# Splitting the expert weight loads into halves of 64 partitions, and taking out 54 products of the unit matrix

## The chip, the cores and the metric

The kernel runs on one core of a Trainium2 chip. Everything is float32. The metric is the device time of one execution in microseconds; the median of three executions before the change is 313.94 us (313.89 to 318.01).

## What is computed

Two blocks follow each other. The first is a DeltaNet recurrence over 768 steps for 4 batches and 8 heads of dimension 48; the second takes its output as 3072 rows of 384 numbers and runs a soft mixture of 8 experts with 4 slots each.

```python
# q, k, v: (4, 8, 768, 48), beta: (4, 8, 768)
for t in range(S):
    y[:, :, t] = einsum('bhd,bhde->bhe', q[:, :, t], state)
    v_old = einsum('bhde,bhd->bhe', state, kt)            # kt: k normalised
    state = state + bt * einsum('bhd,bhe->bhde', kt, vt - v_old)
# x: (3072, 384) from y; phi: (384, 32); w1: (8, 384, 1024); w2: (8, 1024, 384)
logits = x @ phi
d = softmax of logits over the rows;  slot_input = d.T @ x     # 8 experts x 4 slots
slot_out[e] = relu(slot_input[e] @ w1[e]) @ w2[e]
out = (softmax of logits over the slots) @ slot_out
```

## The kernel before

The recurrence is cut into 24 chunks of 32 steps. Six groups of four chunks each are inverted together: `prep` transposes k and q on TensorE (line 533) and forms the Gram products (line 490), `invert` runs an elimination on VectorE (lines 773 and 786), and for the first group a two-halves form with small products (lines 665 and 678). `chunk` then runs the scan: the reads of the state R and Q (line 857), the solve W (line 888), the state update KU (line 903) and the outputs AU (line 934), with copies out of PSUM on ScalarE or VectorE (the helper at lines 326 and 328). Four small DMAs for each chunk (line 945) move the copied outputs Y into X, the tile with one row for each step; there are three Y buffers. After each fourth chunk `route` transposes X (line 961), forms the logits and accumulates the slot inputs (line 1029).

`experts` comes last: the first products with w1 (line 1177), relu, transposes (line 1196), the second products with w2 (line 1208), one product that sums over the parts (line 1225), and 24 output products (line 1237), each scaled on ScalarE or VectorE and stored (line 1250). The second products run over eight parts t of the hidden dimension, four experts beside each other.

The weights are 25 MB. `weights(e)` loads w1 of one expert in three DMAs, each of 128 partitions with 4 KB for each partition (line 1084); `weights2(e)` loads w2 of one expert in four DMAs of 128 partitions with 3 KB each (line 1092). That makes 24 + 32 loads, 29 issued by POOL and 27 by SP. Their buffers ("wt") lie in one large SBUF tile, the arena, in places where the scan's buffers lie earlier: a load can only start when the last user of every buffer under it is done.

The order of all work is written out by hand: every call of `op` gets a number, and `ORDER` lists these numbers, with a letter where the second of an operation's possible engines is meant. `Plan.place` walks through this list once, gives each value its buffer or its PSUM bank, and the program is emitted in that order. So each engine, and each engine's DMA queue, runs its instructions in the order of this list; nothing is reordered later except for what semaphores delay.

At the end of the list of operations stand 54 products of the unit matrix with itself (`warm`, line 1274), numbers 1642 to 1695. Their result is read by nobody. `ORDER` puts 44 of them among the first 533 of its 1696 numbers and the other ten into the routing and expert stage. Each is written as one product and becomes two weight loads and two passes on TensorE.

Of the kernel before, what the change touches and what calls it, by code (L numbers as in the profile page):

```python
# [159 lines left out]
42b 73 8b 9b 31 6b 74 40b 7b 29b 19 1 5b 28 75 368 84 54b 66 10b 72 52b 20 67 1642 1643 1644  # L160
1645 1646 1647 64b 369 377 65b 55b 15b 378 370 87 379 371 86 386 85 372 32b 395 380 381 387 388
396 397 382 1648 1649 1650 1651 1652 76b 1653 1654 78b 77 389 398 373 383 89 390 399 374 404 79b
21 98 409 91 110 88b 99 90 47b 405 406 97 375 22 384 391 392 407 376 385 400 410 411 412 413 414
415 416 417 401 481 393 101b 12b 483 489 482 102b 418 113 96 419 420 1655 1656 421 484 402 485
403 490 422 115b 394 423 109 491 486 487 424 425 426 488 427 492 493 1657 100 494 495 428 103b
429 497 496 499 498 430 431 432 433 434 114b 108 111 112b 500 1658 1659 1660 124b 507 122 120
135 126b 505 501 127b 123 125 508 137b 442 506 509 34b 121 594 502 503 510 435 58b 14 133 44 132
511 150b 161b 436 513 595 437 514 592 438 439 408 440 441 35b 443 444 593 148b 46b 151 144 596
597 1661 1662 1663 1664 1665 1666 1667 1668 1669 445 598 512 139 599 448 446 504 515 136 518 516
520 174 519 463 472 521 522 466 523 464 475 56 524 525 526 527 528 529 530 45 33b 57b 531 1670  # L170
1671 1672 1673 1674 1675 454 532 517 533 467 68 449 145 534 535 457 447 450 451 473 160b 536 537
465 538 468 469 539 476 474 540 541 542 543 455 544 477 478 545 546 458 547 134 548 549 459 550
149 146 175b 456 83 138 602 1048 1036 600 1676 1677 1678 1679 452 453 603 1037 17 71 601 1038
629 460 604 605 551 1039 606 162 552 147 1040 607 610 1041 1042 462 1049 59b 553 554 555 80 1680
1681 1682 1050 163b 556 557 558 559 560 461 561 562 563 564 565 566 16 156 158 567 187b 157 608
186b 568 569 570 1051 159 470 197 1043 69b 609 480 70 1056 618 571 611 81b 616 92 1052 479 104b
94 619 1045 1057 617 173 1532 1058 471 612 620 1060 613 621 614 572 82 622 209b 573 199 1053
210b 624 574 625 168 575 1063 623 170 626 1047 576 615 1683 1055 1054 1116 184 106 577 1059 196
1064 1065 171 578 1078b 169 1066 579 580 581 1684 582 1067 1068 583 1069 627 631 1070 630 632
633 634 635 1071 95b 1072 105 585 636 1044 1079 1080 208b 637 638 116 1062 639 587 1081 640 641  # L180
642 643 584 93b 644 645 646 647 589 211 182 648 181 1082 649 650 651 652 185b 1685 131 1061 1073
703 1083 586 107b 128 1086 183 1087 653 119b 1085 1084 1117 1118 654 655 656 192 117b 657 1076
658 659 660 661 662 663 1131 713 664 665 666 172b 1046 1077 193 1088 1119 740 704 180 130b 705
1120 706 1121 194 714 1123 1122 707 1124 708 709 1132 198 1133 667 129 710 668 195 142 669 670
671 672 673 674 675 1146 628 590 1125 118 222b 207 140 143b 206 1134 155b 721 719 676 205 1135
233 711 23 204 221 1126 677 678 722 1136 712 246b 1074 588 1137 715 247 716 717 679 718 1075
1089 1139 220b 680 720 219 1140 727 729 681 1138 141 1141 728 1147 723 730 682 683 684 1091 1090
591 1092 685 1148 686 1200b 217 1128 724 687 731 732 165 725 726 1161 223 1149 1097 1150 152b
153b 1144 733 1129 1098 688 735 736 167b 689 690 1151 1152 1093 734 1095 154 1153 1094 1096 166b
691 692 693 232 229 1533 231 1154 1127 234b 1162 1099 737 694 1163 1215b 696 698 695 1100b 1101  # L190
738 741 742 164 1102 743 230 744 745 746 747 748 749 750 751 1164 176 1130 739 752 816 1109 753
1110 216 1165 700 1166 697 228 218 817 1168 256b 241 754 1111 235b 1169 1155 177b 1170 178 1167
755 756 240 1143 1201 1156 1202 243 242 814 189b 1158 757 758 759 760 761 1142 762 763 764 765
766 1230 822 1203 767 768 1171 188b 815 270b 1204 1174 818 823 819 245b 701 824 1172 1205 1208
820 769 825 257 1175 283b 821 1209 1207 770 1145 1206 1216 1173 1245 771 1217 252 259b 826 244b
254 772 773 774 775 255 1159 776 1218 777 778 1210 830 827 779 828 1219 780 829 1157 258b 201b
1220 781 1223 1103 699 782 1160 783 784 785 786 787 788 831 1224 1180 1105 1178 1222 1221 1225
832 1181 1231 1112 179b 1106 253 1176 1212 1179 190b 266 840 833 265 838 1232 789 1113 790 791
214b 702 792 294b 1177 841 839 292b 282 1233 293 793 1234 271b 794 268 795 834 835 836 842 843
1235 796 851 1228 844 797 846 191 1236 1237 279 202 1284 847 845 1229 798 837 799 800 1246 1107  # L200
269b 1182 1247 801 295 1211 281b 802 1248 848 803 1108 804 805 267 1299 1183 1184 849 852 853
1185 1249 854 855 856 857 203 858 850 859 860 861 862 1238 1250 927 1253 807 1254 1252 1251 806
1285 1226 278 1286 863 864 865 866 867 1186 868 869 870 871 872 873 1214 874 875 876 877 1239
307 305 277 200 928 808 264 276 809 225b 811 1227 1287 925 1288 926 1289 1240 288 289 280 290
1255 1292 929 1291 304b 933 1293 1290 930 1213 291 878 931 301 879 934 1300 932 880 1301 881 882
215b 883 884 885 303 886 887 888 1314 889 306b 890 1242 891 237 1294 941 935 1189 942 1241 302
1302 936 1243 300 937 1303 1304 1190 1244 250b 226 938 939 1114 892 940 943 1115 212b 1306 1307
1305 1308 962 893 239b 894 895 1315 896 1316 897 249b 898 899 900 213 901 227 238 1296 944 810
813 949 1257 248 951 1317 1309 950 952 902 945 1318 236b 251b 812 903 904 946 1258 947 905 953
954 955 1398 906 224 957 1319 262 907 313 1320 958 908 956 909 1321 1256 1329b 1193 1368 910 948  # L210
911 1194 912 1195 1383 1259 913 959 1330 1331 914 915 916 960 963 964 965 966 967 968 969 970
971 972 1322 1332 1260 1333 917 1297 1261 1334 1336 1335 275 1264 1262 973 1323 1369 974 1324
1370 975 976 977 978 979 980 981 316b 918 1337 1371 272b 982 317 1312 983 984 985 986 987 988
274 961 1263 1265 1372 1373 1298 989 990 1375 261 312b 1313 1295 1266 1374 1376 1384 1385 1311
991 992 1267 1268 993 994 995 996 315b 997 998 999 1000 1001 1187 1310 1377 1002 1269 1003 1196
1004 920 919 314b 1328 922 1386 1338 1387 1327 1326 921 1388 287b 1339 1005 286 1389 319b 1390
1270 1325 1391 263 1191 1399 260b 320b 1006 285b 1342 1400 1378 1392 1007 1008 1341 1340 1009
1010 1011 1192 1012 1013 1014 296b 1413 1401 1402 1403 1343 1404b 1393 299 1273 924 1015 1346
1016 1406 1017 1018 273b 1405 923 1414 1415 1019 298b 1020 1021 1022 1023 1024 1025 297b 1380
1407 1381 1416 1452 1026 1274 309b 1408 1348 1417 1027 1347 1418 1382 308 1419 1275 1420b 1379  # L220
310 1421 318 1349b 1029b 1453 1454 1031 1422 1028 1032 1394 1396 284 1271 1035 1455 1030b 321
1423b 1034b 1344 1456 1457 324 1467b 1395 1412 328 1411 1460 330b 1345b 1350 323 1458b 1397 1459
1033 329b 311b 1468 1351 325b 1104 1461 1352 1409 1469 1470 1475 1462 1410 1353 1471 1427 1482b
1354 1472 1476 1473 1357 1424 1358 1474b 327b 331b 1425 332b 1426 326b 1463 1466 1483 1359 1484
322 1477 1497b 1485 1490 1355 1486b 1276 1487 1488b 1478 1491 1489 1428 1492b 1498 1432 1430
1431 1499 1197 1500 1502 1481 1479 335 1501b 1433b 1503 1429b 1464 1361 1465 1504 1480 1434 1495
1505 1435b 1506 1507 334 333 338 1496 1445 1494 1436 1493 339b 336 1437 1438 1686 1277 1512 1439
1508 1510 337 1441 1360 1513b 1509b 1687 1688 1511 1278 1514 1515 1516 1517 1525 1442 1443 1518
1521 343b 1519 1534 342 1444 1535 341b 1536 1522 1537 1538 1689 1690 1691 1692 340b 345b 1523
1524 1541 1198 1693 1694 346b 344 1695 350 353b 1542b 349 351 354 347 1545 355 352 348 1543 357b  # L230
363b 359b 367b 358 1546 1544 1547 356 1188 360 1279 365 364b 361b 1549 1553 1272 1526 1280 1548
1282 1551 1550b 1559 1356 1560 1440 362 1199b 366b 1446 1281 1552 1362 1554 1555 1557 1556b 1561
# [10 lines left out]
def kernel(  # L243
# [12 lines left out]
    P = 128  # L256
# [4 lines left out]
    NWARM = 54  # L261
# [1078 lines left out]
```

## Time and profile before

| | value |
|---|---|
| median of three executions | 313.94 us |
| profiled execution | 322.0 us, of which 320.2 us from its first to its last instruction |
| mean granted TensorE clock in it | 0.894 of full speed |
| TensorE matmul / weight loads busy | 268.8 us (84%) / 216.4 us (68%), 6080 each |
| VectorE, ScalarE, POOL busy | 221.2 us (69%), 191.0 us (60%), 119.3 us (37%) |
| line 1084 (w1) loads, issue on POOL / on SP | 11 of 531 ns / 13 of 445 ns (medians) |
| line 1092 (w2) loads, issue on POOL / on SP | 18 of 537 ns / 14 of 428 ns (medians) |
| line 1084 / 1092, issue to landing | median 6.8 us (3.9 to 10.3) / 8.5 us (4.6 to 14.8) |
| line 1274, unit-matrix products | 108 passes, 19.5 us busy |

In the profile PE is TensorE's matmul side and PEld its weight loads; DVE is VectorE, ACT ScalarE, POOL GpSimd and SP SyncE. A "q" behind an engine's name means its sequencer, which issues DMAs. A matmul's end is modelled, so the busy time of PE overstates its work. The clock is given as a share of full speed, and the DMA share is the mean busy share of the core's 16 DMA engines[...]. The chain of waits follows the work that ended last back to what released it, step by step; "issue" in it is time in which the engine waited for nothing that the profile shows.

### The profile page before, as it was taken

To read this page: it belongs to the slowest core of one execution; us is meant where nothing else is said; L and a number is where in the kernel's file an instruction comes from. 1 tells how busy PE (TensorE), PEld (TensorE's weight loads), DVE (VectorE), ACT (ScalarE), POOL (GpSimd) and SP (SyncE) were. 2 spreads that over 40 slices of the span, in tenths; PEclk is the share of its full clock that TensorE was granted. 3 is DMA by queue.
4 is the path that set the end of the run, shared out by engine and by line. 5 is a ranking of instruction groups with operands and counts; after the bars stand their busy time and mean duration, and the time that the engine had idled before them with its cause. 6 is when DMAs were issued, how large, how long until landed. Compare 5 with 4: busy or idle time off the path is not lost.

```text
span 320.2 us, 14453 instructions
## 1 busy us (share of the span) xinstructions
PE 268.8 (84%) x6080; PEld 216.4 (68%) x6080; DVE 221.2 (69%) x609; ACT 191.0 (60%) x473; POOL 119.3 (37%) x252
## 2 busy tenths in 40 slices
PE   4998689959899899995999597698798988899890
PEld 4887578857778778884878586576686875333460
DVE  5489996797689999999799999847532544012530
ACT  2545565883799898987798887386442132211362
POOL 8659492126614274445405162222000234300032
PEclk9999956995999999996999989789986999999955
DMA  8968511343555546644528249959992699993195
GB/s 129 154 120 165 90 42 35 58 76 58 96 88 100 99 69 118 114 81 76 102 42 162 49 107 265 217 104 323 316 279 49 198 354 398 377 356 147 68 326 198
DMA packets 87472, 49.66 MB, mean 155 GB/s; under 512 B 77280, under 2 KB 79200, under 8 KB 87408
## 3 DMA queue, kind: packets, MB, share of 16 engines
q1 hardware_dynamic: 78176, 28.41, 40.0%
q0 software_dynamic: 7056, 19.93, 21.8%
q8 instruction: 48, 0.79, 1.1%
q10 hardware_dynamic: 2176, 0.39, 0.9%
q14 instruction: 16, 0.13, 0.1%
HBM read 39.47 MB, written 4.72 MB: 138 GB/s over the span
## 4 chain that ended last, share of the span: by engine, by line
PE 57%; DVE 18%; ACT 8%; issue 7%; DMA 6%; POOL 2%; SPq 0%; POOLq 0%; ACTq 0%; DVEq 0%
PE banks L857 9%; PE banks L888 6%; PE banks L903 6%; PE banks L934 5%; PE banks L490 5%; ACT arena L326 5%; DMA arena<-in_moe_w_dram 4%; PE banks L533 4%; PE banks L1274 4%; PE banks L1237 4%; DVE arena L696 3%; PE banks L961 2%; DVE arena L773 2%; DVE arena L786 2%; PE banks L1177 2%
## 5 line engine op out<-in xcount | busy, mean ns | idle before, releaser
L326 ACT ACTIVATE arena<-banks 64x384 f32<-64x384 f32 (+4 forms) x205 | 98.8, 505 | 71.8 <-PE banks L903 22.1
L786 DVE TENSOR_TENSOR arena<-arena 128x31 f32<-128x31 f32 (+15 forms) x155 | 53.1, 343 | 4.2
L773 DVE TENSOR_TENSOR arena<-arena 128x60 f32<-128x60 f32 (+9 forms) x150 | 52.0, 347 | 3.9
L452 POOL DMA_DIRECT2D arena<-in_v_dram x49 | 28.7, 589 | 59.3 <-DVE arena L773 23.0
L857 PE MATMUL banks<-arena 128*32 128x96 f32 x1440 | 44.6, 271 | 6.2 <-DVE arena L509 3.6
L857 PEld LDWEIGHTS banks<-arena 128*32 128x32 f32 x1440 | 35.1, 121 | 12.7 <-issue 7.9
L452 POOL DMA_DIRECT2D arena<-in_q_dram x58 | 33.8, 588 | 14.7 <-PE banks L533 14.1
L328 DVE COPY arena<-banks 64x384 f32<-64x384 f32 (+3 forms) x24 | 13.6, 577 | 31.8 <-PE banks L1196 13.9
L888 PE MATMUL banks<-arena 64*64 64x48 f32 x768 | 29.7, 230 | 5.6 <-issue 2.3
L888 PEld LDWEIGHTS banks<-arena 64*64 64x64 f32 x768 | 27.1, 146 | 10.5 <-issue 3.5
L903 PE MATMUL banks<-arena 32*128 32x96 f32 x736 | 29.4, 296 | 5.0 <-issue 3.0
L533 PE MATMUL banks<-ident,arena 128*128 128x128 f32 x192 | 29.4, 292 | 4.6 <-DVE par L392 4.6
L846 ACT ACTIVATE arena<-arena,nTall 128x48 f32<-128x48 f32 x136 | 32.1, 322 | 0.1
L903 PEld LDWEIGHTS banks<-arena 32*128 32x128 f32 x736 | 25.0, 199 | 9.5 <-issue 4.5
L934 PE MATMUL banks<-arena 64*64 64x48 f32 x736 | 27.8, 227 | 3.1 <-issue 3.1
L562 ACT ACTIVATE arena<-arena,par 128x256 f32<-128x256 f32 x45 | 29.8, 698 | 0.3 <-DVE arena L790 0.2
L934 PEld LDWEIGHTS banks<-arena 64*64 64x64 f32 x736 | 25.0, 142 | 6.4 <-issue 4.1
L490 PE MATMUL banks<-arena 64*64 64x128 f32 (+1 forms) x896 | 26.2, 261 | 2.5 <-DVE arena L509 1.5
L533 PEld LDWEIGHTS banks<-ident,arena 128*128 128x128 f32 x192 | 22.2, 148 | 7.1 <-issue 5.3
L490 PEld LDWEIGHTS banks<-arena 64*64 64x64 f32 x896 | 22.1, 136 | 4.8 <-ACT arena L326 3.3
L878 DVE TENSOR_TENSOR arena<-arena,banks 128x384 f32<-128x384 f32 x23 | 12.6, 549 | 16.0 <-PE banks L857 10.2
L1274 PE MATMUL banks<-ident 128*128 128x128 f32 x108 | 19.5, 332 | 4.3 <-DVE arena L509 3.5
(141 smaller groups left out, 349.9 us busy)
## 6 DMA issues: line engine op xcount, KB each, us to landing
arena<-in_moe_w_dram POOLq DMA_DIRECT2D x18, 384.0 KB, 8.2
arena<-in_moe_w_dram SPq DMA_DIRECT2D x13, 512.0 KB, 7.4
arena<-in_moe_w_dram POOLq DMA_DIRECT2D x11, 512.0 KB, 5.8
arena<-in_moe_w_dram SPq DMA_DIRECT2D x14, 384.0 KB, 9.3
arena<-arena SPq DMA_DIRECT2D x92, 48.0 KB, 3.2
arena<-in_k_dram SPq DMA_DIRECT2D x88, 48.0 KB, 3.0
out_dram<-arena SPq DMA_DIRECT2D x15, 192.0 KB, 2.1
arena<-in_q_dram POOLq DMA_DIRECT2D x58, 48.0 KB, 3.1
```

The lines of the kernel that those rows point to most:

```text
L326: AC.activation(dst, src, ACT.Copy)
L452: dge[e].dma_start(out=sb(x, U, pad)[hs[h], :, 0:D], in_=src.rearrange("b (g h) s d -> h s (b g) d", h=4)[h, cc * C:(cc + 1) * C])
L490: PE.matmul(t[hp_[hp], g, b * P:b * P + m], lhsT=kt[rs_[g], b, 0, h2].rearrange("p h t -> p (h t)"), rhs=rhs, start=True, stop=True, skip_ ...
L533: PE.transpose(t[:, b, :], m[:, b, :], ident)
L773: nc.vector.tensor_tensor(o.rearrange("p (i k) -> p i k", k=m), t[:, j, 0:m].unsqueeze(1).broadcast_to([P, a1 - a0, m]), s[:, i, j].unsque ...
L786: nc.vector.tensor_tensor(d, d, o, op=ALU.subtract)
L846: AC.activation(t[:, b, g], t[:, b, g], ACT.Copy, scale=f[:, b, g:g + 1])
L857: PE.matmul(t[hs[h], b], lhsT=m[:, b, a, hs[h]], rhs=s[:, h, b], start=(a == 0 or b == 0), stop=False, skip_group_check=True)
L888: PE.matmul(t[hp_[i], b, g], lhsT=m[hp_[i], g, b], rhs=r[hp_[i], b, g], start=True, stop=True, skip_group_check=True)
L903: PE.matmul(banks[:, h, b * G * D:(b + 1) * G * D], lhsT=m[hs[h], b], rhs=r[hs[h], b], start=(cc == 0 and b == 0), stop=True, skip_group_c ...
L934: PE.matmul(t[hp_[i], b, g], lhsT=m[hp_[i], g, b], rhs=r[hp_[i], b, g], start=(cc == 0 and b == 0 and g == 0), stop=True, skip_group_check ...
L1274: PE.matmul(ps(wm, P), lhsT=ident, rhs=ident, start=True, stop=True)
```

## The change

Each weight load is issued as two DMAs, one for partitions 0 to 63 and one for 64 to 127, one after the other on the same queue. The number of unit-matrix products is set to zero, and their numbers are taken out of `ORDER`; the order of the other numbers is the same.

```diff
-1645 1646 1647 64b 369 377 65b 55b 15b 378 370 87 379 371 86 386 85 372 32b 395 380 381 387 388
-396 397 382 1648 1649 1650 1651 1652 76b 1653 1654 78b 77 389 398 373 383 89 390 399 374 404 79b
...
+42b 73 8b 9b 31 6b 74 40b 7b 29b 19 1 5b 28 75 368 84 54b 66 10b 72 52b 20 67 64b 369 377 65b
+55b 15b 378 370 87 379 371 86 386 85 372 32b 395 380 381 387 388 396 397 382 76b 78b 77 389 398
...
-    NWARM = 54
+    NWARM = 0
...
         for i in range(NKT):
             def ld(eng, i=i, x=x):
-                dge[eng].dma_start(out=sb(x, NKT, F)[:, i],
-                                   in_=moe_w1[e].rearrange("(p k) f -> p k f", k=NKT)[:, i])
+                for h in (slice(0, 64), slice(64, P)):
+                    dge[eng].dma_start(out=sb(x, NKT, F)[h, i],
+                                       in_=moe_w1[e].rearrange("(p k) f -> p k f", k=NKT)[h, i])
...
         for i in range(4):
             def ld(eng, i=i, x=x):
-                dge[eng].dma_start(out=sb(x, NFC, Dm)[:, 2 * i:2 * i + 2],
-                                   in_=moe_w2[e].rearrange("(p t) d -> p t d", t=NFC)[
-                                       :, 2 * i:2 * i + 2])
+                for h in (slice(0, 64), slice(64, P)):
+                    dge[eng].dma_start(out=sb(x, NFC, Dm)[h, 2 * i:2 * i + 2],
+                                       in_=moe_w2[e].rearrange("(p t) d -> p t d", t=NFC)[
+                                           h, 2 * i:2 * i + 2])
```

Lines after the list move up by three in the new file, and those below the first load by one or two.

More of the change, by code (lines that the diff above doesn't have):

```diff
@@ L159 @@
 24b 4b 13b 25 27b 26 2b 3b 18b 37b 38 39b 11b 36 50b 63 60 51b 0 48b 49b 61 62 30b 43b 41b 53b
-42b 73 8b 9b 31 6b 74 40b 7b 29b 19 1 5b 28 75 368 84 54b 66 10b 72 52b 20 67 1642 1643 1644
-1645 1646 1647 64b 369 377 65b 55b 15b 378 370 87 379 371 86 386 85 372 32b 395 380 381 387 388
-396 397 382 1648 1649 1650 1651 1652 76b 1653 1654 78b 77 389 398 373 383 89 390 399 374 404 79b
-21 98 409 91 110 88b 99 90 47b 405 406 97 375 22 384 391 392 407 376 385 400 410 411 412 413 414
-415 416 417 401 481 393 101b 12b 483 489 482 102b 418 113 96 419 420 1655 1656 421 484 402 485
@@ L165 @@
[L165 to L230, printed above, removed]
@@ L231 @@
-363b 359b 367b 358 1546 1544 1547 356 1188 360 1279 365 364b 361b 1549 1553 1272 1526 1280 1548
-1282 1551 1550b 1559 1356 1560 1440 362 1199b 366b 1446 1281 1552 1362 1554 1555 1557 1556b 1561
-1558 1562 1563 1564 1565 1566 1363 1520 1364 1539 1567 1366 1365 1540 1283 1568 1569 1570 1573
-1576 1582 1447 1367b 1448 1450 1579 1571 1574b 1451b 1577 1580 1572 1588 1597 1585 1578 1575b
-1600 1591 1583 1594 1581 1449 1586 1603 1615 1589b 1590 1592 1595 1606 1609 1612 1598b 1601 1527
-1599 1621 1587b 1584 1528 1624 1618 1604b 1607 1530 1627 1610 1529 1613 1602 1531 1593 1616b
@@ L237 @@
-1619 1608 1605b 1636 1630 1622b 1639 1596b 1623 1625b 1628 1631 1633 1614b 1611b 1634 1620 1637
-1640 1635b 1632b 1641 1638 1629 1626 1617b
+42b 73 8b 9b 31 6b 74 40b 7b 29b 19 1 5b 28 75 368 84 54b 66 10b 72 52b 20 67 64b 369 377 65b
+55b 15b 378 370 87 379 371 86 386 85 372 32b 395 380 381 387 388 396 397 382 76b 78b 77 389 398
+373 383 89 390 399 374 404 79b 21 98 409 91 110 88b 99 90 47b 405 406 97 375 22 384 391 392 407
+376 385 400 410 411 412 413 414 415 416 417 401 481 393 101b 12b 483 489 482 102b 418 113 96 419
@@ new lines @@
+420 421 484 402 485 403 490 422 115b 394 423 109 491 486 487 424 425 426 488 427 492 493 100 494
+495 428 103b 429 497 496 499 498 430 431 432 433 434 114b 108 111 112b 500 124b 507 122 120 135
+126b 505 501 127b 123 125 508 137b 442 506 509 34b 121 594 502 503 510 435 58b 14 133 44 132 511
+150b 161b 436 513 595 437 514 592 438 439 408 440 441 35b 443 444 593 148b 46b 151 144 596 597
+445 598 512 139 599 448 446 504 515 136 518 516 520 174 519 463 472 521 522 466 523 464 475 56
+524 525 526 527 528 529 530 45 33b 57b 531 454 532 517 533 467 68 449 145 534 535 457 447 450
@@ new lines @@
+451 473 160b 536 537 465 538 468 469 539 476 474 540 541 542 543 455 544 477 478 545 546 458 547
+134 548 549 459 550 149 146 175b 456 83 138 602 1048 1036 600 452 453 603 1037 17 71 601 1038
+629 460 604 605 551 1039 606 162 552 147 1040 607 610 1041 1042 462 1049 59b 553 554 555 80 1050
+163b 556 557 558 559 560 461 561 562 563 564 565 566 16 156 158 567 187b 157 608 186b 568 569
+570 1051 159 470 197 1043 69b 609 480 70 1056 618 571 611 81b 616 92 1052 479 104b 94 619 1045
+1057 617 173 1532 1058 471 612 620 1060 613 621 614 572 82 622 209b 573 199 1053 210b 624 574
@@ new lines @@
+625 168 575 1063 623 170 626 1047 576 615 1055 1054 1116 184 106 577 1059 196 1064 1065 171 578
+1078b 169 1066 579 580 581 582 1067 1068 583 1069 627 631 1070 630 632 633 634 635 1071 95b 1072
+105 585 636 1044 1079 1080 208b 637 638 116 1062 639 587 1081 640 641 642 643 584 93b 644 645
+646 647 589 211 182 648 181 1082 649 650 651 652 185b 131 1061 1073 703 1083 586 107b 128 1086
+183 1087 653 119b 1085 1084 1117 1118 654 655 656 192 117b 657 1076 658 659 660 661 662 663 1131
+713 664 665 666 172b 1046 1077 193 1088 1119 740 704 180 130b 705 1120 706 1121 194 714 1123
@@ new lines @@
+1122 707 1124 708 709 1132 198 1133 667 129 710 668 195 142 669 670 671 672 673 674 675 1146 628
+590 1125 118 222b 207 140 143b 206 1134 155b 721 719 676 205 1135 233 711 23 204 221 1126 677
+678 722 1136 712 246b 1074 588 1137 715 247 716 717 679 718 1075 1089 1139 220b 680 720 219 1140
+727 729 681 1138 141 1141 728 1147 723 730 682 683 684 1091 1090 591 1092 685 1148 686 1200b 217
+1128 724 687 731 732 165 725 726 1161 223 1149 1097 1150 152b 153b 1144 733 1129 1098 688 735
+736 167b 689 690 1151 1152 1093 734 1095 154 1153 1094 1096 166b 691 692 693 232 229 1533 231
@@ new lines @@
+1154 1127 234b 1162 1099 737 694 1163 1215b 696 698 695 1100b 1101 738 741 742 164 1102 743 230
+744 745 746 747 748 749 750 751 1164 176 1130 739 752 816 1109 753 1110 216 1165 700 1166 697
+228 218 817 1168 256b 241 754 1111 235b 1169 1155 177b 1170 178 1167 755 756 240 1143 1201 1156
+1202 243 242 814 189b 1158 757 758 759 760 761 1142 762 763 764 765 766 1230 822 1203 767 768
+1171 188b 815 270b 1204 1174 818 823 819 245b 701 824 1172 1205 1208 820 769 825 257 1175 283b
+821 1209 1207 770 1145 1206 1216 1173 1245 771 1217 252 259b 826 244b 254 772 773 774 775 255
@@ new lines @@
+1159 776 1218 777 778 1210 830 827 779 828 1219 780 829 1157 258b 201b 1220 781 1223 1103 699
+782 1160 783 784 785 786 787 788 831 1224 1180 1105 1178 1222 1221 1225 832 1181 1231 1112 179b
+1106 253 1176 1212 1179 190b 266 840 833 265 838 1232 789 1113 790 791 214b 702 792 294b 1177
+841 839 292b 282 1233 293 793 1234 271b 794 268 795 834 835 836 842 843 1235 796 851 1228 844
+797 846 191 1236 1237 279 202 1284 847 845 1229 798 837 799 800 1246 1107 269b 1182 1247 801 295
+1211 281b 802 1248 848 803 1108 804 805 267 1299 1183 1184 849 852 853 1185 1249 854 855 856 857
@@ new lines @@
+203 858 850 859 860 861 862 1238 1250 927 1253 807 1254 1252 1251 806 1285 1226 278 1286 863 864
+865 866 867 1186 868 869 870 871 872 873 1214 874 875 876 877 1239 307 305 277 200 928 808 264
+276 809 225b 811 1227 1287 925 1288 926 1289 1240 288 289 280 290 1255 1292 929 1291 304b 933
+1293 1290 930 1213 291 878 931 301 879 934 1300 932 880 1301 881 882 215b 883 884 885 303 886
+887 888 1314 889 306b 890 1242 891 237 1294 941 935 1189 942 1241 302 1302 936 1243 300 937 1303
+1304 1190 1244 250b 226 938 939 1114 892 940 943 1115 212b 1306 1307 1305 1308 962 893 239b 894
@@ new lines @@
+895 1315 896 1316 897 249b 898 899 900 213 901 227 238 1296 944 810 813 949 1257 248 951 1317
+1309 950 952 902 945 1318 236b 251b 812 903 904 946 1258 947 905 953 954 955 1398 906 224 957
+1319 262 907 313 1320 958 908 956 909 1321 1256 1329b 1193 1368 910 948 911 1194 912 1195 1383
+1259 913 959 1330 1331 914 915 916 960 963 964 965 966 967 968 969 970 971 972 1322 1332 1260
+1333 917 1297 1261 1334 1336 1335 275 1264 1262 973 1323 1369 974 1324 1370 975 976 977 978 979
+980 981 316b 918 1337 1371 272b 982 317 1312 983 984 985 986 987 988 274 961 1263 1265 1372 1373
@@ new lines @@
+1298 989 990 1375 261 312b 1313 1295 1266 1374 1376 1384 1385 1311 991 992 1267 1268 993 994 995
+996 315b 997 998 999 1000 1001 1187 1310 1377 1002 1269 1003 1196 1004 920 919 314b 1328 922
+1386 1338 1387 1327 1326 921 1388 287b 1339 1005 286 1389 319b 1390 1270 1325 1391 263 1191 1399
+260b 320b 1006 285b 1342 1400 1378 1392 1007 1008 1341 1340 1009 1010 1011 1192 1012 1013 1014
+296b 1413 1401 1402 1403 1343 1404b 1393 299 1273 924 1015 1346 1016 1406 1017 1018 273b 1405
+923 1414 1415 1019 298b 1020 1021 1022 1023 1024 1025 297b 1380 1407 1381 1416 1452 1026 1274
@@ new lines @@
+309b 1408 1348 1417 1027 1347 1418 1382 308 1419 1275 1420b 1379 310 1421 318 1349b 1029b 1453
+1454 1031 1422 1028 1032 1394 1396 284 1271 1035 1455 1030b 321 1423b 1034b 1344 1456 1457 324
+1467b 1395 1412 328 1411 1460 330b 1345b 1350 323 1458b 1397 1459 1033 329b 311b 1468 1351 325b
+1104 1461 1352 1409 1469 1470 1475 1462 1410 1353 1471 1427 1482b 1354 1472 1476 1473 1357 1424
+1358 1474b 327b 331b 1425 332b 1426 326b 1463 1466 1483 1359 1484 322 1477 1497b 1485 1490 1355
+1486b 1276 1487 1488b 1478 1491 1489 1428 1492b 1498 1432 1430 1431 1499 1197 1500 1502 1481
@@ new lines @@
+1479 335 1501b 1433b 1503 1429b 1464 1361 1465 1504 1480 1434 1495 1505 1435b 1506 1507 334 333
+338 1496 1445 1494 1436 1493 339b 336 1437 1438 1277 1512 1439 1508 1510 337 1441 1360 1513b
+1509b 1511 1278 1514 1515 1516 1517 1525 1442 1443 1518 1521 343b 1519 1534 342 1444 1535 341b
+1536 1522 1537 1538 340b 345b 1523 1524 1541 1198 346b 344 350 353b 1542b 349 351 354 347 1545
+355 352 348 1543 357b 363b 359b 367b 358 1546 1544 1547 356 1188 360 1279 365 364b 361b 1549
+1553 1272 1526 1280 1548 1282 1551 1550b 1559 1356 1560 1440 362 1199b 366b 1446 1281 1552 1362
@@ new lines @@
+1554 1555 1557 1556b 1561 1558 1562 1563 1564 1565 1566 1363 1520 1364 1539 1567 1366 1365 1540
+1283 1568 1569 1570 1573 1576 1582 1447 1367b 1448 1450 1579 1571 1574b 1451b 1577 1580 1572
+1588 1597 1585 1578 1575b 1600 1591 1583 1594 1581 1449 1586 1603 1615 1589b 1590 1592 1595 1606
+1609 1612 1598b 1601 1527 1599 1621 1587b 1584 1528 1624 1618 1604b 1607 1530 1627 1610 1529
+1613 1602 1531 1593 1616b 1619 1608 1605b 1636 1630 1622b 1639 1596b 1623 1625b 1628 1631 1633
+1614b 1611b 1634 1620 1637 1640 1635b 1632b 1641 1638 1629 1626 1617b
```

## Prediction

> **What bounds the kernel now.** I read the page's clock and DMA rows first, then the busy times in stretches of 4 us, then the chain of waits, and last the DMA issues of the tail. The profiled execution took 322.0 us (span 320.2), 2.6% above the median of 313.94; I work out differences in it and add them to the median.
>
> From the page: the granted clock and the DMA share in 40 slices of 8 us, the unit-matrix products, and the queue that brings instructions.
>
> ```profile
> PEclk9999956995999999996999989789986999999955
> DMA  8968511343555546644528249959992699993195
> ...
> L1274 PE MATMUL banks<-ident 128*128 128x128 f32 x108 | 19.5, 332 | 4.3 <-DVE arena L509 3.5
> ...
> q8 instruction: 48, 0.79, 1.1%
> ```
>
> The products (54, each recorded as two passes) are 19.5 us of TensorE time. The clock halves in slices 6, 10 and the last two. Memory is loaded in slices 22 to 36, where the weights arrive. Stretches of 4 us (PE, weight loads, DVE, ACT, POOL busy; clock; DMA share; GB/s):
>
> ```profile
> 40.00:44.00 4.00, 3.25 (x41) 3.14 (x41) 3.52 (x11) 2.30 (x7) 3.94 (x6) 0.56 0.21 43
> 52.00:56.00 4.00, 4.00 (x77) 3.60 (x78) 1.74 (x5) 1.09 (x2) 1.90 (x4) 0.73 0.25 53
> ...
> 72.00:76.00 4.00, 3.27 (x60) 2.70 (x61) 2.38 (x8) 1.34 (x6) 3.18 (x11) 0.50 0.38 62
> ...
> 204.00:208.00 4.00, 2.68 (x47) 2.58 (x46) 3.43 (x10) 0.49 (x1) 0.00 (x0) 0.54 1.10 216
> ...
> 268.00:272.00 4.00, 3.26 (x30) 2.33 (x29) 2.02 (x8) 0.17 (x1) 2.46 (x5) 1.00 1.04 408
> ```
>
> VectorE is at least 85% busy in most stretches from 16 to 52 us and from 92 to 208: it bounds the scan. TensorE decides where VectorE has holes (52 to 92) and from 208 on. From 255 the loads of w2 run beside TensorE's last stage at about 400 GB/s. The chain (start, length):
>
> ```profile
> 41.37 2.86 PE banks L1274 x12
> ...
> 52.16 1.71 PE banks L1274 x8
> ...
> 202.24 3.08 issue
> ...
> 227.13 2.33 issue
> ...
> 239.55 2.06 issue
> ...
> 278.76 13.78 DMA arena<-in_moe_w_dram
> 292.58 4.71 PE banks L1208 x55
> ```
>
> The last load of w2 ends at 292.5, and the second products, the fold and 24 stores hang on it. It is a near tie: TensorE itself stood only 0.5 us before 292.58. The three "issue" pieces lie about 127 passes, or a multiple of that, apart; 127 passes are 254 instructions. The DMA view of 252 to 292.6 us:
>
> ```profile
> DMA packets 4969, 14.40 MB, mean 355 GB/s; under 512 B 1646, under 2 KB 1646, under 8 KB 4963
> ...
> arena<-in_moe_w_dram POOLq DMA_DIRECT2D x18, 384.0 KB, 8.2
> arena<-in_moe_w_dram SPq DMA_DIRECT2D x14, 384.0 KB, 9.3
> ```
>
> [...] after TensorE's idle at 68 to 72 us the next stretches are at 0.50. [...]
>
> **The split.** 29 POOL loads and 27 SP loads become 58 and 54 of half the size. Bytes and order stay.
>
> *Issue.* POOL: 29 x 0.54 us = 15.6 us more, SP: 27 x 0.43 = 11.6. POOL has nothing behind its last loads before the store at 302 us, but its last five (277.6 to 280.2) become ten and end near 283. Both queues then issue 384 KB in 1.07 us (POOL) and 0.86 us (SP), together 800 GB/s, twice what lands: hidden by the transfers themselves; without that cover it costs 2.7 us. On SP the moves L945 and v loads queue behind the w1 parts, each 0.43 us later per part; the waits for them are ACT's output copies (three Y buffers) and L961. In the compiled instruction list a queue's DMA waits for the one eight before it, so half as many bytes are in flight per queue; 8 x 192 KB on two queues is 3 MB, 7.9 us at 400 GB/s, as much as a load takes now: nothing.
>
> *Rate.* Unknown[...]. The two queues are at different places, so an even half on one may run beside an odd half on the other. [...]
> - Tail: 14.40 MB take 51.4 us instead of 40.6: +10.8 (0 to +26). Of it about 3.3 return: the last load, of two of the eight parts t of one expert, is needed by 16 of the 55 passes that now follow it (2 parts x 4 experts x 2 passes), and the others can go ahead (4.71 x 39/55). TensorE then waits in pieces, with a halved clock now and then: +1. Net +8.5 (0 to +24).
> - w1 stage, 186 to 252 us: 23 parts (12.06 MB) and 57 transfers of 48 KB. At 166 GB/s (the stretch 8 to 12 us, small transfers only, engines full) the small ones need 17 us; the weights 30 us at 400, 43 at 280[...]. Sum 47, 60 or 73 of 66 us. At 280 the slack is nearly gone, so moves, v loads and instruction blocks come later here and there: I take +3 (-5 to +10; the gain is below).
>
> **The removal.** 216 instructions and 108 passes go from TensorE; the PSUM bank of every other product stays as it was. *Gain:* on the chain lie 12.8 us of them (4.0%), but what follows decides. The 12 at 5.7 us free transposes whose copy waits for ACT until 7.5: under 1 us. Those of 12 to 40 us lie beside VectorE's unbroken work: 0; next late is VectorE. Those at 41.4, 52.2 and 60.1 (2.86 + 1.71 + 0.86) are before the first chunks, where VectorE stands idle 4.0 us in 52 to 62: at most 4 us. Those of 261 to 272 lie beside the w2 transfers: 0. *Cost:* [...] At 5.7 us a pass took 213 ns (2.56/12) and at 27.9 us 112 ns (0.67/6), though the clock row shows 1.00 at both: I read the start as half rate, too. The rate doubled while they ran, so without them TensorE may stay at half rate for a stretch longer at the start and around 52. A chunk at half clock is 4 us dearer (L888 1.95 for 0.93, L903 1.97 for 1.07, L857 twice 1.44 for 0.80, L934 1.88 for 1.06). The trace also shows recovery by chunk work alone in about 5 us (147 to 152, 206 to 210). Range -4 to +5; I take -1.
>
> **Sum:** 8.5 + 3 - 1 = +10.5 us, 322.0 to 332.5 in the profiled terms, and 313.9 to **325 us** for the median.
>
> **Rivals.**
> - [...] +24 in the tail, +7 in the w1 stage (73 - 66), -1: +30, **344 us**. [...]
> - *No limit:* 400 GB/s stay, issue is hidden, clock cost and gain cancel: **314 us**. [...]
> - *Faster, by shorter blocking.* The stalls of 0.97, 3.08, 0.97, 2.33 and 2.06 us from 197 to 242 (9.4 us) are instruction blocks behind weights. If an engine finishes one load's share before it turns to the block, halves cut this wait to half: -4.7, and the halved clock after each stall (0.54 at 204 to 208) goes too, -1; with the products' 3 us: **305 us**. It decides only if the rate stays above about 350 GB/s; below it the queue is longer and eats the gain.
> - *The change acts on the clock alone*, more than I take: +5, 319 us.
>
> **How the numbers follow.** Middle rate 0.43 (316 to 334), [...] no limit with the clock case 0.18 (309 to 321), shorter blocking 0.12 (301 to 308). A measurement of this kernel tells about 2% from no change: 307.7 and 320.2. Slower: 0.27 + 0.33 of the middle case + 0.02 = 0.62. Same: 0.10 + 0.11 + 0.02 = 0.23. Faster: 0.05 + 0.10 = 0.15. The range is 307 to 346, leaving out about 0.12 below and 0.08 above.
>
> **What would show it.** Right: w2's transfers at 220 to 320 GB/s with a DMA share near 1, the last load landing 8 us or more after the end of the first products' first half than now, and PE waits for weights before L1207 (L1208 now). Wrong: 400 GB/s in the tail (then the rivals with the rate kept); "issue" pieces under 1 us between 190 and 250 (shorter blocking); clock stretches of 0.50 before 60 us longer than now with VectorE waiting for TensorE there (the clock cost is larger than I took).

## Result and the profile after

The changed kernel took **345.23 us** (median of 4 executions, 343.29 to 346.32) beside 315.98 us for the kernel before (median of 4): 29 us more, a ratio of 1.096 (95% interval 1.090 to 1.101). The forecast was 325 us; the time lies at the upper end of its range, where the rival at 344 us put it.

The profiled execution took 343.29 us (span 341.4). Executions of one kernel differ by some per cent, the ratio compares the quicker ones of both kernels, and the profiled one of before, 322.0 us, was a long one: the two profiles differ by 21.3 us and the medians by 29.2. The page of the changed kernel: clock, DMA share and GB/s in 40 slices (8.5 us each), then the second products of the experts and the w2 loads (busy us, mean ns of one, then idle time before them and what ended most of it), last the two queues' w2 issues (count, KB each, median us to landing).

```profile
PEclk9998656967999999999996976969899989678995
DMA  8978511444555455345571999999999999998087
GB/s 134 140 127 139 84 39 27 78 74 75 101 96 107 74 108 107 72 78 98 92 136 19 217 194 173 194 217 221 208 209 216 226 242 250 241 239 206 2 298 256
...
L1091 POOL DMA_DIRECT2D arena<-in_moe_w_dram x36 | 18.8, 525 | 29.2 <-DMA arena<-in_moe_w_dram 21.9
...
L1207 PE MATMUL banks<-arena 128*32 128x384 f32 x128 | 16.1, 613 | 16.0 <-DMA arena<-in_moe_w_dram 16.0
...
arena<-in_moe_w_dram POOLq DMA_DIRECT2D x36, 192.0 KB, 10.1
...
arena<-in_moe_w_dram SPq DMA_DIRECT2D x28, 192.0 KB, 16.4
```

The DMA share stands at 0.9 or more in 14 slices in a row, and in all of them less than 255 GB/s are moved; before, the page has 354 to 398 in four slices of the tail. Half the bytes of a load now take longer to land than the whole took (10.1 and 16.4 us against 8.2 and 9.3). TensorE waits 16.0 us for weights ahead of its second products, where it waited 0.5 us:

```profile
L1208 PE MATMUL banks<-arena 128*32 128x384 f32 x128 | 11.5, 488 | 0.5 <-DMA arena<-in_moe_w_dram 0.5
```

Stretches of 4 us of the changed kernel (PE, weight loads, DVE, ACT, POOL; clock; DMA share; GB/s):

```profile
252.00:256.00 4.00, 2.99 (x62) 2.33 (x59) 2.04 (x6) 0.40 (x2) 2.55 (x5) 1.00 1.00 210
...
268.00:272.00 4.00, 2.52 (x20) 0.84 (x20) 2.83 (x8) 1.41 (x6) 1.83 (x4) 1.00 1.03 224
...
292.00:296.00 4.00, 0.00 (x0) 0.00 (x0) 0.00 (x0) 0.00 (x0) 1.61 (x4) 0.68 1.04 248
```

At 268 to 272 us the same DMA share (1.03, before 1.04) carries 224 GB/s instead of 408: a busy share told here how long packets were under way, not how much they carried. At 292 TensorE, VectorE and ScalarE all stand still. The whole stretch from 252 us to the landing that the last products wait for, by the DMA view of 252 to 314 us:

```profile
DMA packets 6828, 14.54 MB, mean 235 GB/s; under 512 B 3539, under 2 KB 3539, under 8 KB 6822
```

That is about as many bytes as before (14.40 MB), in 62.0 us instead of 40.6. And the end of the chain of waits, after it the end of the scan in the chain of before:

```profile
257.02 2.76 PE banks L806 x32
...
266.76 14.98 DMA arena<-in_moe_w_dram
281.80 17.20 DMA arena<-in_moe_w_dram
299.07 14.87 DMA arena<-in_moe_w_dram
314.07 6.32 PE banks L1207 x55
```

```profile
255.57 2.76 PE banks L809 x32
```

The last products of the scan start only 1.5 us later (257.02 against 255.57). The load that the last products of the experts wait for lands at 313.9 us against 292.5, +21.4; behind it come 27.5 us against 27.7. So the loss between these two profiles, 21.2 us of span, is the transfer of w2. The profile of before was itself long ahead of the tail, though, so this pair hides part of what the w1 stage costs; the section "Which stage" has that.

That load is not the last to land, as the prediction took it to be. Behind it SP issues four more halves of w2, the last at 308.6 us, and they land by 316.3 us; from 312 to 316 us 154 GB/s are still moved. Before, two more loads came behind it and landed by 294.5 us.

### The profile page after: what moved, and what is told of

The parts are those of the page before. It is cut to its first block, busy times and chain, and to the rows that moved or that the text cites. A ratio compares the mean times of both kernels' runs of the same rounds, so it can differ in the third digit from the quotient of the medians.

```text
span 341.4 us, 14343 instructions
## 1 busy us (share of the span) xinstructions
PE 261.5 (77%) x5972; PEld 206.7 (61%) x5972; DVE 221.2 (65%) x609; ACT 190.7 (56%) x473; POOL 134.5 (39%) x281
## 4 chain that ended last, share of the span: by engine, by line
PE 48%; DMA 19%; ACT 11%; DVE 9%; issue 8%; SPq 3%; POOL 0%; POOLq 0%; ACTq 0%; DVEq 0%
DMA arena<-in_moe_w_dram 14%; PE banks L854 8%; PE banks L900 7%; PE banks L885 6%; PE banks L487 5%; ACT arena L323 5%; PE banks L530 5%; PE banks L931 5%; DMA arena<-in_k_dram 4%; ACT arena L843 3%; PE banks L958 2%; PE banks L1207 2%; DVE arena L693 2%; DVE arena L875 1%; DMA arena<-arena 1%
## 5 line engine op out<-in xcount | busy, mean ns | idle before, releaser
L783 DVE TENSOR_TENSOR arena<-arena 128x31 f32<-128x31 f32 (+15 forms) x155 | 53.0, 342 | 4.2
L770 DVE TENSOR_TENSOR arena<-arena 128x60 f32<-128x60 f32 (+9 forms) x150 | 52.0, 347 | 3.9
L854 PEld LDWEIGHTS banks<-arena 128*32 128x32 f32 x1440 | 36.0, 122 | 15.6 <-ACT arena L323 7.1
L530 PE MATMUL banks<-ident,arena 128*128 128x128 f32 x192 | 31.7, 310 | 6.8 <-DMA arena<-in_k_dram 4.8
L885 PE MATMUL banks<-arena 64*64 64x48 f32 x768 | 30.5, 232 | 6.8 <-issue 3.1
L885 PEld LDWEIGHTS banks<-arena 64*64 64x64 f32 x768 | 27.6, 147 | 11.2 <-issue 4.1
L487 PE MATMUL banks<-arena 64*64 64x128 f32 (+1 forms) x896 | 28.6, 277 | 3.7 <-DVE arena L506 2.0
L530 PEld LDWEIGHTS banks<-ident,arena 128*128 128x128 f32 x192 | 24.1, 158 | 10.3 <-issue 5.8
L1091 POOL DMA_DIRECT2D arena<-in_moe_w_dram x36 | 18.8, 525 | 29.2 <-DMA arena<-in_moe_w_dram 21.9
L931 PE MATMUL banks<-arena 64*64 64x48 f32 x736 | 27.8, 227 | 1.0 <-issue 1.0
L1207 PE MATMUL banks<-arena 128*32 128x384 f32 x128 | 16.1, 613 | 16.0 <-DMA arena<-in_moe_w_dram 16.0
L487 PEld LDWEIGHTS banks<-arena 64*64 64x64 f32 x896 | 24.2, 149 | 6.2 <-ACT arena L323 3.0
L931 PEld LDWEIGHTS banks<-arena 64*64 64x64 f32 x736 | 25.0, 142 | 4.5 <-issue 2.6
## 6 DMA issues: line engine op xcount, KB each, us to landing
arena<-in_moe_w_dram POOLq DMA_DIRECT2D x36, 192.0 KB, 10.1
arena<-in_moe_w_dram SPq DMA_DIRECT2D x28, 192.0 KB, 16.4
```

The source lines that it names most:

```text
L487: PE.matmul(t[hp_[hp], g, b * P:b * P + m], lhsT=kt[rs_[g], b, 0, h2].rearrange("p h t -> p (h t)"), rhs=rhs, start=True, stop=True, skip_ ...
L530: PE.transpose(t[:, b, :], m[:, b, :], ident)
L770: nc.vector.tensor_tensor(o.rearrange("p (i k) -> p i k", k=m), t[:, j, 0:m].unsqueeze(1).broadcast_to([P, a1 - a0, m]), s[:, i, j].unsque ...
L783: nc.vector.tensor_tensor(d, d, o, op=ALU.subtract)
L854: PE.matmul(t[hs[h], b], lhsT=m[:, b, a, hs[h]], rhs=s[:, h, b], start=(a == 0 or b == 0), stop=False, skip_group_check=True)
L885: PE.matmul(t[hp_[i], b, g], lhsT=m[hp_[i], g, b], rhs=r[hp_[i], b, g], start=True, stop=True, skip_group_check=True)
```

## Experiments

Ratios are against the kernel before, run on the same chip beside each kernel. "Products out" is `NWARM = 0` with the numbers taken out of `ORDER`, as in the change.

### Each part alone

Products out, loads whole:

```diff
-    NWARM = 54
+    NWARM = 0
```

> Only the 54 products are taken out; the loads keep 128 partitions. Theory A (the halves cost the time, by the rate of a transfer into 64 partitions): the time stays near that of before, 310 to 319 us (ratio 0.99 to 1.016), and the w2 loads run near 400 GB/s. Rival B (the products kept TensorE's clock up and their loss is a large part of the +9.6%): 322 us or more, with more stretches at clock 0.50 before 90 us.

Loads split at partition 64, products kept:

```diff
+                for h in (slice(0, 64), slice(64, P)):
+                    dge[eng].dma_start(out=sb(x, NKT, F)[h, i],
...
+                for h in (slice(0, 64), slice(64, P)):
+                    dge[eng].dma_start(out=sb(x, NFC, Dm)[h, 2 * i:2 * i + 2],
...
```

> Only the loads are split into halves of 64 partitions; the 54 products stay. Theory A: 340 to 348 us (ratio 1.08 to 1.11), w2 at 220 to 250 GB/s. Rival B: 330 us or less, since the products are there.

Products out: 321.60 us, 1.011 (1.001 to 1.020). Split: 342.81 us, 1.086 (1.077 to 1.095). Nearly all of the loss is the split's. In stretches of 4 us of the kernel with the products out, the tail flows as before:

```profile
264.00:268.00 4.00, 2.56 (x24) 0.84 (x20) 2.39 (x8) 1.71 (x7) 1.60 (x4) 1.00 1.01 396
268.00:272.00 4.00, 3.30 (x19) 1.78 (x23) 1.35 (x6) 0.00 (x0) 1.61 (x3) 0.72 1.04 406
272.00:276.00 4.00, 4.00 (x38) 0.99 (x32) 0.00 (x0) 0.69 (x1) 0.00 (x0) 0.85 1.02 400
```

About 400 GB/s, but the clock falls to 0.72 and 0.85 where the first products of the experts begin; with the products it stood at 1.00 there.

### Twice the transfers, but over all partitions

Each load is cut along its row instead: two transfers over 128 partitions, 2 KB (w1) or 1.5 KB (w2) of each row. First with the products out, then with them.

```diff
-                for h in (slice(0, 64), slice(64, P)):
-                    dge[eng].dma_start(out=sb(x, NKT, F)[h, i],
+                for h in (slice(0, HF), slice(HF, F)):
+                    dge[eng].dma_start(out=sb(x, NKT, F)[:, i, h],
...
+                for t in (2 * i, 2 * i + 1):
+                    dge[eng].dma_start(out=sb(x, NFC, Dm)[:, t],
...
```

> As the changed kernel (no products, every load issued as two), but each half has all 128 partitions and half of the row (2 KB for w1, 1.5 KB for w2). Theory A: the rate comes back to 350 GB/s or more in the tail and the time to 311 to 321 us. Rival C (twice as many DMAs, with eight in flight per queue and twice the issue time, are the cost): 335 us or more, w2 below 300 GB/s.

> Products kept, each load in two transfers over all 128 partitions, half a row each. If the number of transfers, the issue time and the eight in flight per queue cost nothing and the products are worth 1%: 0.995 to 1.005 of the kernel before, 312 to 317 us, tail at 370 to 400 GB/s. If the doubled issue costs: 1.01 or more, 318 us and up.

Products out 1.015 (1.008 to 1.023), with products 1.003 (0.998 to 1.008). The same count of DMAs and the same bytes in each, at hardly any cost; in the traces of before and of the change at most eight DMAs of a queue are between issue and landing at once. The DMA view of the first, 262 to 284 us:

```profile
DMA packets 4131, 8.17 MB, mean 371 GB/s; under 512 B 663, under 2 KB 3031, under 8 KB 4129
```

371 GB/s where whole loads give 378 in the same stretch (products out). Doubled issue and half-size transfers were rightly costed at about nothing.

### Even and odd partitions

Products out; the halves are every second partition, 64 partitions in each as in the change.

```diff
-                for h in (slice(0, 64), slice(64, P)):
+                for h in (slice(0, P, 2), slice(1, P, 2)):
```

> As the changed kernel, but the two halves are the even and the odd partitions, 64 each with whole rows. Theory A in its narrow form (what counts is which partitions[...]): 311 to 321 us, w2 near 400 GB/s. Rival D (any transfer of 64 partitions is slow, whichever they are): 340 us or more, w2 near 235 GB/s.

374.42 us, 1.187: no expectation of the time held. Stretches of 4 us and pieces of the chain of this kernel:

```profile
296.00:300.00 4.00, 2.79 (x17) 1.50 (x16) 2.04 (x7) 0.57 (x2) 2.39 (x5) 0.89 1.03 413
300.00:304.00 4.00, 3.79 (x21) 1.90 (x24) 0.86 (x5) 0.00 (x0) 2.33 (x5) 0.57 1.02 399
```

```profile
213.87 5.47 DMA arena<-in_moe_w_dram
221.98 3.31 DMA arena<-in_moe_w_dram
229.54 4.00 DMA arena<-in_moe_w_dram
237.29 3.53 DMA arena<-in_moe_w_dram
```

Where transfers flow, they flow at 399 to 413 GB/s. The time is lost elsewhere, in waits for weights that the change does not have. VectorE's elimination (L770 and L783) waits 30.1 us for them, in the change not at all, and the first w2 load is issued at 288 us, not at 257. The transposes between the experts' products (L1195) wait 19.9 us for them, where those of the change wait 2.5 us, for ScalarE alone. Why these waits arise was not shown. So the time of this kernel says nothing about the split, only its rate does.

### Which stage

Products out, and only w2 or only w1 split at partition 64; the other loads whole.

> Products out, only the w2 loads in two halves on one queue, as in the change; w1 loads whole. Theory P and Q alike, if the cost is the rate in the tail: 14.4 MB at 235 instead of 400 GB/s are 61 instead of 36 to 41 us, +20 to +25 over the kernel with only the products out, 340 to 346 us. Rival R (w1's later arrival sets off half of the loss): 330 to 335 us.

> Products out, only the w1 loads in two halves, w2 whole. If the tail carries the cost: within 0 to +5 us of the kernel with only the products out, 320 to 327 us, with tail transfers at 380 to 410 GB/s again. Rival R: 330 to 335 us.

Only w2: 337.60 us, 1.073 (1.060 to 1.086). Only w1: 324.62 us, 1.028 (1.012 to 1.043). The second lies within its first expectation, the first 2 us below its own. Stretches of the kernel with only w1 split show the switch:

```profile
252.00:256.00 4.00, 3.07 (x71) 2.59 (x72) 1.10 (x4) 0.60 (x1) 1.09 (x3) 1.00 1.09 226
...
272.00:276.00 4.00, 3.40 (x27) 2.67 (x31) 1.25 (x6) 0.00 (x0) 1.50 (x3) 1.00 1.05 407
```

While w1's halves move, 226 GB/s; with w2's whole loads, 407. Added up: the products 0.8% (mean of two measurements, 1.011 and, below, 1.005), w1 2.0% more, w2 6.5% more, 9.3% in all beside the 9.6% of the change. The intervals of these ratios are one per cent wide or more, so the parts are rough.

The traces show w1's part more closely, as the time from SP's first w1 load to the last products of the scan (L806 or L809). SP's w1 loads and these products in the kernel with row halves and the products kept, then SP's w1 loads in the change, whose last products of the scan stand at 257.02:

```profile
L1085 SPq DMA_DIRECT2D arena<-in_moe_w_dram x26: 327/432/1413, 185.2 to 236.9; - x26
249.21 2.76 PE banks L809 x32
...
L1082 SPq DMA_DIRECT2D arena<-in_moe_w_dram x26: 465/593/1652, 185.2 to 247.0; - x26
```

That is 64 us with w1 over all partitions and 72 us with w1 cut at partition 64. In the four traces with w1 cut there it is 70.8 to 72.2 us; in the fifteen others, the kernel with even and odd partitions left aside, it is 63.3 to 68.9, 65.8 in the mean. So the split of w1 costs about 6 us, and the profile of before, with 68.9 the longest of the fifteen, hides half of it.

### Opposite halves side by side

My middle rate rested on halves of different sides running together. Here that is brought about: products out, w1 whole, and of every w2 load the lower half goes to SP and the upper half to POOL, 32 on each.

```diff
-                for h in (slice(0, 64), slice(64, P)):
+                for eng, h in (("SP", slice(0, 64)), ("POOL", slice(64, P))):
```

> Products out, w1 loads whole, each w2 load in two halves, but partitions 0 to 63 always on SP and 64 to 127 always on POOL, 32 loads on each queue, so that opposite halves are asked for at the same time. Theory P (which partitions a transfer covers limits its rate, and the halves come close together in place only if they stand in both queues at once; this was the ground of my middle rate): with opposite halves always side by side the tail rises to 350 to 400 GB/s and the time to that of the kernel with only the products out, 318 to 326 us. Rival Q (a 64-partition transfer is slow whatever runs beside it): 220 to 260 GB/s as in the change, the last load near 312 us, 338 to 346 us.

333.44 us, 1.062 (1.045 to 1.079), between the two expectations. In stretches of 4 us, both queues full:

```profile
264.00:268.00 4.00, 2.51 (x24) 1.29 (x16) 2.33 (x6) 1.12 (x5) 1.76 (x4) 1.00 1.02 290
...
272.00:276.00 4.00, 3.79 (x36) 0.84 (x28) 0.00 (x0) 0.77 (x2) 0.52 (x1) 0.99 1.05 281
```

The DMA view of 262 to 298 us gives a mean of 265 GB/s (and 248 for halves following each other on one queue, only w2 split). The queues do not keep step: POOL issues its last half at 286.7 us and SP at 296.6, so in the end lower halves move alone. While both move, from 264 to 292 us, the stretches carry 248 to 290. Company helps, and falls far short of 400.

The change itself, with the order of the two halves turned round on POOL alone:

```diff
-                for h in (slice(0, 64), slice(64, P)):
+                for h in ((slice(0, 64), slice(64, P)) if eng == "SP" else (slice(64, P), slice(0, 64))):
```

> The changed kernel with POOL issuing the upper half of each load first and SP the lower half first; sizes, counts and queues as in the change. If the chance order of halves in the two queues made the change slow: between the kernel with opposite halves in the two queues (1.06) and the change (1.095), 333 to 340 us. If the order does not matter, since each queue alternates halves anyway and holds eight: as the change, 1.085 to 1.10, 342 to 347 us, tail at 235 to 250 GB/s.

343.68 us, 1.094 (1.084 to 1.104), 239 GB/s in 262 to 306 us: as the change. Which half goes first made no difference.

### Side, number or memory

Products out, w1 whole, w2 in other pieces:

```diff
-                for h in (slice(0, 64), slice(64, P)):
+                for h in (slice(32, 96), slice(0, 32), slice(96, P)):
```

> Products out, w1 loads whole, each w2 load in three: partitions 32 to 95 (64 partitions, both sides of 64), then 0 to 31 and 96 to 127. Theory S (what counts is which side of partition 64 a transfer covers): half the bytes, in the middle parts, flow at 370 to 400 GB/s and the rest at about 240, together near 300 GB/s; 14.4 MB take 49 us instead of 36 to 41 (whole) and 61 (cut at 64), 1.03 to 1.055 of the kernel before. Theory N (what counts is how many partitions a transfer covers): the middle parts stay at 240 and the parts of 32 are no faster, at most 240 GB/s together, 1.07 or more.

```diff
+                for h in (slice(0, 32), slice(32, 64), slice(64, 96), slice(96, P)):
```

> Products out, w1 loads whole, each w2 load in four of 32 partitions, one after the other on its queue. Theory S: 32 partitions lie on one side as 64 do, so 225 to 260 GB/s as with halves, 1.07 to 1.08 of the kernel before, plus at most 3 us for 128 issues instead of 64. Theory N: the rate falls on, to 120 to 180 GB/s, the last load lands 20 us or more after that of the halves, 1.13 or more.

With a middle part: 333.44 us, 1.064 (1.060 to 1.069), 247 GB/s in 256 to 292 us; the side theory had expected near 300 and a ratio of at most 1.055, the number theory at most 240 and at least 1.07, and both missed. Quarters: 339.81 us, 1.081 (1.055 to 1.107), 248 GB/s in the same stretch, as the side theory had it; the number theory had expected 120 to 180, and missed. So one more question was put to the rows' place in memory, and three shapes were measured unmixed:

```diff
-                for h in (slice(0, 64), slice(64, P)):
+                for q in (0, 1):
+                    h = slice(64 * q, 64 * q + 64)
                     dge[eng].dma_start(out=sb(x, NFC, Dm)[h, 2 * i:2 * i + 2],
                                        in_=moe_w2[e].rearrange("(p t) d -> p t d", t=NFC)[
-                                           h, 2 * i:2 * i + 2])
+                                           q:P:2, 2 * i:2 * i + 2])
```

> Products out, w1 loads whole, each w2 load in two: partitions 0 to 63 receive the even rows of the weights, 64 to 127 the odd rows, so the weights of the experts' second stage are in the wrong partitions. Destinations as in the kernel with only w2 split, source rows as in the kernel with even and odd partitions. Theory D (the destination's partitions decide): 235 to 260 GB/s, 1.065 to 1.08 of the kernel before. Theory M (the place of the rows in the device's memory decides, a half of an expert's matrix against every second row): 370 to 410 GB/s, 1.00 to 1.025.

```diff
-                for h in (slice(0, 64), slice(64, P)):
+                for h in (slice(0, 64),):
```

The other two have `slice(32, 96)` and `slice(0, P, 2)` there. All three leave the other half of w2 out, and each was run once.

> Products out, w1 loads whole, of each w2 load only partitions 0 to 63; the upper half of the experts' second weights is not loaded, 6.3 MB less. A measure of the rate of this one shape: 200 to 235 GB/s while the queues are full, under theory D as under M.

> As the kernel with the lower half only, but partitions 32 to 95 are loaded and the others are not. If what counts is that both sides of partition 64 are reached: 350 to 410 GB/s. If any block of 64 neighbouring partitions is slow: 200 to 260 GB/s. If M, 200 to 260 too.

> As the two before, but the even partitions (and even rows) are loaded and the odd ones are not. 350 to 410 GB/s while the queues are full, under D as under M; 200 to 260 if the rate in the kernel with even and odd partitions came from the pair of them.

Lower and upper half of the partitions with even and odd rows as source: 340.18 us, 1.095 (1.079 to 1.111; 1.077 by the medians), 240 GB/s in 262 to 298 us, beside 248 where each half has its own rows as source (only w2 split). So the destination decided here, not the memory read. The three shapes, one stretch of 4 us each; lower half, middle, even partitions:

```profile
256.00:260.00 4.00, 2.24 (x26) 1.57 (x26) 2.23 (x5) 1.30 (x4) 0.00 (x0) 1.00 1.02 204
```

```profile
256.00:260.00 4.00, 2.93 (x42) 2.18 (x39) 2.80 (x7) 1.86 (x6) 0.00 (x0) 1.00 0.93 330
```

```profile
252.00:256.00 4.00, 2.87 (x98) 2.06 (x97) 1.31 (x4) 2.24 (x7) 1.53 (x3) 1.00 0.99 305
```

One side alone carries 204 GB/s with the engines full, within its expectation. Partitions 32 to 95, as many and as neighbouring, carry 330 at a share of 0.93, by proportion about 355 for a full share (an estimate); a load then lands in 4.5 us at the median instead of 9.3. The even partitions carry 305 at 0.99. Both were expected at 350 or more and missed it: they lie far above the lone side, yet below the 400 of whole loads, and why is open. So what counted first is whether both sides of partition 64 are reached (330 and 305 GB/s against 204). This also goes far to explain the miss of the kernel with middle parts: half its bytes at 355 and half at 204, one after the other, are 1/(0.5/355 + 0.5/204) = 259 GB/s, and 247 were measured; I had put 240 for a lone side, which is the rate of a mixture.

Opposite halves at once, one in each queue, moved 30% more than one side alone (265 against 204 GB/s), and whole loads 378 to 408.

### The products, early and late

Loads whole as before; in one kernel the first 44 products do nothing, in the other (`i >= 44`) the last ten; and once more all 54 out, on the same chip.

```diff
-        def warm(e, wm=wm):
+        def warm(e, wm=wm, i=i):
+            if i < 44:
+                return
```

> The loads whole as before; of the 54 products of the unit matrix the first 44 (those before 80 us) are out, the 10 of 261 to 272 us stay. Theory E (the products' removal costs about 1% because they keep the clock before the first chunks): 1.007 to 1.014 of the kernel before, 317 to 321 us. Theory L (it is the last ten, which keep the clock ahead of the first products of the experts): 0.995 to 1.004, 313 to 318 us. My prediction's term (gain about cancels cost, -1 us): 0.99 to 1.00.

> The loads whole as before; of the 54 products the last ten are out, the first 44 stay. Theory E: 0.997 to 1.003 of the kernel before, 314 to 318 us. Theory L: 1.007 to 1.014, 317 to 321 us. My prediction's term put 0 here, beside the w2 transfers.

> All 54 products out, loads whole, beside the two partial removals on one chip. Theories E and L: 1.007 to 1.014 of the kernel before, and about the product of the two partial ratios. If the earlier 1.011 was chance: 0.997 to 1.003.

Early out: 0.996 (0.992 to 1.000). Late out: 1.014 (1.005 to 1.022). All out: 1.005 (0.999 to 1.012), between its two expectations. By these ratios it is the ten before the experts' products that earn their place, but the size is uncertain: by the medians of all executions the late ones are worth 0.5% (318.64 us out, 317.00 before), and taking all 54 out cost 1.1% and 0.5% in two measurements. In the profiles with all out, the clock is below 1 where those products begin (0.72 above; 0.73 at 268 to 272 us in the second measurement). The profiled execution with only the late ones out, its quickest, shows 1.00 throughout 252 to 300 us, so the link by way of the clock is argued, not shown.

No version beat the kernel before beyond its interval; the nearest is the one without the early products.

## Why the prediction was wrong

The direction, the place and the kind of cause (transfers to one side of partition 64 are slower: 204 GB/s alone, where whole loads move about 400) were right. The rate in the tail, and a return of time behind it, were not.

- **The rate, the step that failed.** The prediction put the 14.40 MB of the tail at 51.4 us, which is 280 GB/s. That was an assumption of mine with nothing measured under it: in the kernel before every weight load covers 128 partitions. It took two opposite halves side by side to run at 400, as whole loads do; with opposite halves in the two queues the rate was 265, and 204 for one side alone. If the halves differ half of the time, the mean of these two is 1/(0.5/265 + 0.5/204) = 231 GB/s, an estimate whose half stays an assumption; 235 were measured from 252 to 314 us. Tail: +21.4 us instead of +10.8.
- **The return of 3.3 us** did not come. The prediction let 39 of the last 55 passes go ahead of the late load. But TensorE ran these products in the order of the list, and the awaited load is needed early: the second products go through the parts t and, for each part, through four experts, and it was the fourth of the last 32 products (64 passes) that waited. In the timeline of the changed kernel:

```profile
314.07 6.62 PE L1207 MATMUL banks<-arena 128*32 128x384 f32 x57 [5.38 <-DMA arena<-in_moe_w_dram]
...
320.53 0.49 PE L1207 MATMUL banks<-arena 128*32 128x384 f32 x1
```

  All 58 passes behind the wait start after the landing, as 58 did before (57 and one, from 292.58). The loads that land still later held none of them up.
- **The clock behind the wait**, +1: the 55 passes in the chain took 6.32 us, not 4.71, at a clock of 0.74 and 0.83; the whole remainder behind that landing stayed (27.5 and 27.7 us); in the profile of before the output stage ran at a clock of 0.50 from 304 us on.
- **The w1 stage**, +3 (-5 to +10): about +6, by the traces and by the kernel with only w1 split (2.0% over the products out, with intervals as wide as the effect). In the profile of the change the DMA share is at 1 or above in most stretches from 188 to 256 us, at about 210 GB/s, and the slack before the tail is gone; the +7 of the rival at 344 us fits better.
- **The removal**, -1: the early products came out near it (-0.4%, 1.3 us). "Those of 261 to 272 lie beside the w2 transfers: 0" was wrong by its ratio: +1.4%. With the split in both, the products out cost 1.0% (1.096 against 1.086), in two sets of runs whose intervals overlap.
- **Issue, rotation and count of transfers**, costed at nothing: right (1.003 for row halves).
- **Shorter blocking**: no sign of it. The "issue" pieces of 0.9 us or more from 195 to 253 us add up to 9.6 us, before to 9.4; and the rate, 210 to 235 GB/s, was far below the 350 that it was to need, an estimate of mine. One packet of the instruction queue, 0.02 MB, falls beside the longest stall of before (202 to 206 us); that it waited behind weights was not shown.
- **The rival at 344 us** came within 2 us, in part by luck: it had the tail slower than it was (+24 even after a return of 3.3 us that did not come, against +21.4), which about made up for the gain of 1 us that it counted on from the removal. Its rate, too, was an assumption with nothing measured under it.

## What to carry to other kernels

Cut a load along its row, not across its partitions: two transfers over all partitions cost 0.3% here, two of 64 each 8.6%. Don't credit two half-wide transfers with the full rate because they are in flight together (265 GB/s here, whole loads about 400): measure the pair before any reasoning about mixtures. And a late load was waited for by everything behind its first user on TensorE, whether it needed the load or not: 58 passes here.

## What the hardware showed beyond that

- Transfers to 64 partitions run at 204 GB/s or at 330 (share 0.93), by nothing but which 64: 0 to 63, or 32 to 95. The even ones alone ran at 305.
- The DMA share is 1.02 to 1.05 alike at 204 GB/s (lower halves alone), 224 (the change), 290 (opposite halves) and 408 (whole loads).
- Quarters of 32 partitions, 96 KB each, move as fast as halves (248 GB/s both). Opposite halves are little faster one in each queue (265) than following each other on both (248); why two sides in flight don't add up to 400 is open.
- Ten idle products of the unit matrix, 3.0 us of busy TensorE beside transfers, were worth 1.4% by the ratio (0.5 to 2.2), 0.5% by the medians.
